# Slots on both sides of the dense blocks, earlier return of the output weights' buffers, earlier projections

## The chip, the cores and the metric

The kernel runs on one core of a Trainium2 chip. The metric is the device time of one launch in microseconds. Engines are named as the profile names them: PE (TensorE matmul) and PEld (its weight load), DVE (VectorE), ACT (ScalarE), POOL (GpSimd) and SP (SyncE, which here only issues transfers).

## The reference

All data is float32, 2048 tokens of width 512. The output is `x + A(xn) + B(xn)` with `xn = layernorm(x)`.

```python
# A: 32 heads of width 16, one shared key and value head
q = (xn @ wq).reshape(B, S, H, Dh).transpose(0, 2, 1, 3); k = xn @ wk; v = xn @ wv
p = softmax(einsum("bhqd,bkd->bhqk", q, k) * Dh ** -0.5)
A = einsum("bhqk,bkd->bhqd", p, v).transpose(0, 2, 1, 3).reshape(B, S, H * Dh) @ wo
# B: product-key experts, 64 x 64 of them, 32 heads
q1, q2 = split(einsum("nd,dhc->nhc", xn, w_q))            # 128 wide each
t1, i1 = top2(q1 @ k1.T); t2, i2 = top2(q2 @ k2.T)
top_s, top_e = top2(t1[:, None] + t2[None, :])            # of the 4 candidates
g = softmax(top_s)
act = gelu(einsum("nd,nhkd->nhk", xn, u[top_e]))          # tanh form
B = einsum("nhk,nhk,nhkd->nd", g, act, v[top_e])
```

So each token has 64 experts (32 heads, two each) out of 4096.

## The kernel before

**Attention sets the pace.** Tokens are 16 tiles of 128, in four groups. After a start stage (norms, transposes, projections) the main loop runs over `half` = 256 pairs `d` and a few more. A pair is two chunks of 128 keys for one unit; a unit is one block of 512 queries and four heads, so a unit is 8 pairs and a query block 64. Query blocks come in the order `QB = (0, 1, 3, 2)`. In a pair PE makes scores (`scores`, L325), ACT their exponentials (L328), and PE the products with the values (`pv`, L339). `i = 2 * d` counts chunks.

**The order is written out by hand.** Inside the loop every engine executes its instructions in the order in which the program emits them. `att_steps` emits, for each pair: stored-up transfers, half of the scores, the value products of the pair before, then `mid`, the other half of the scores, at most one output projection, and `fill`. `fill` advances the score thread, a generator whose yields carry costs, up to a budget that grows evenly over the loop.

**Experts are done in two ways.** Token groups 0 and 1 gather expert rows: this work is cut into 512 slots (`NSL`), each one expert of one token tile. A slot is a gather of 128 rows of 1024 floats by POOL (L957), a dot with the tokens on DVE (L969), and, four slots at a time, a short gate chain (L978 to L980 on DVE, tanh L985 on ACT, weight L992), then a weighted add into the token tile on DVE (L1004). Groups 2 and 3 are done densely, each in a dense block of the score thread: the last routing items (scores L527, top values L540 and L542, `batch` L567 to L639), transposes of the routing (L744), a one-hot stage that builds gate matrices (DVE L767 to L770, PE L801, ACT L806, then transfers to and from `d_g`), and 32 dense steps of activations (L719), GELU and gate on DVE and ACT (L886 to L907), and sums over experts (PE L843, DVE L846).

**Stages of a dense block.** `dense_on` is 0 outside; 3 from the third routing item of the block's last chunk; 2 from the end of the routing transposes, that is in the one-hot stage; 3 again from two steps before the one-hot stage's end; 1 from the end of dense step 4; and 0 when the block ends.

**Pace of the slots.** `pos` is the number of slots due. Each pair adds to it by the stage, `todo` is what of it is not yet dotted, and `mid` emits those dots, then a limited number of adds (`sums`), then up to four gathers.

```python
if d < half * 3 // 4:
    pos += 2.1 if len(IDX) < NC * TPH else (1.7, 2.5, 1.4, 0.0)[dense_on[0]]
else:
    pos += max(0.0, NSL - pos) / max(half - 4 - d, 1) if dense_on[0] < 3 else 0.0
```

**The gather ring.** Slots' rows lie in a ring of `NGB` = 12 buffers. `gathers` issues while `g_next < a_next + NGB - lent`, so a buffer comes free by a slot's add. The output weights `wo` of attention (two buffers' worth) borrow from the same ring: `lent` becomes 2 at `i % 128 == 124` (pairs 62, 126, 190), and `load_wo` loads them a few pairs into the next query block.

**Output projections.** `block_out` (PE L432, DVE add L436) projects one token tile of a finished query block; there are four to a block. For blocks 0 and 2 of the order two are emitted in the dense block (steps 2 and 3), the others from `i % 128 >= HOLD` on; for block 1 they come at every other pair as soon as the tiles are in place. Each charges 3.6 to the score thread's budget. `lent` returns to 0 at `HOLD + 8` (for block 1 at 30), and the last 30 chunks have the limit reduced once more.

Of the kernel before, what the change touches and what calls it, by code (L numbers as in the profile page):

```python
# [33 lines left out]
NC = 8  # L34
TPH = GT
# [11 lines left out]
LIMIT2 = 25000.0  # L47
C_IN = 0.7978845608028654
C_CUB = 0.044715 * C_IN
HOLD = 56  # L50
MOST = 4.0
UNIT = 0.235

# [2 lines left out]
def tile_kernel(ctx, tc, x, wq, wkv, wo, wqT, kT, uv, ub, vb, out):  # L56
# [246 lines left out]
    def load_q(u, rows=True, maxima=True):  # L303
        qb, hg = units[u]
        qa = qa_bufs[u % 2]
        QA[u] = qa
        c = slice(qb * 512, (qb + 1) * 512)
        for b in range(2):
            h0 = 4 * hg + 2 * b
            o = 64 * b  # L310
            if maxima:
                nc.sync.dma_start(raw(qa[o + 48:o + 50]), d_m[:, h0:h0 + 2, c])
            if rows:
                src = [d[h0 * DH:(h0 + 2) * DH, c].rearrange("(h r) n -> r h n", r=DH) for d in (d_qh, d_ql)]
                nc.sync.dma_start(raw(qa[o:o + 16]), src[0])
                nc.sync.dma_start(raw(qa[o + 16:o + 32]), src[0])
                nc.sync.dma_start(raw(qa[o + 32:o + 48]), src[1])
# [3 lines left out]
    def scores(u, kc, i):  # L321
        p = stile("sc")
        for b in range(2):
            o = 64 * b
            nc.tensor.matmul(p[:, b, :], kaug[o:o + 64, kc * P:(kc + 1) * P], QA[u][o:o + 64, i, :],  # L325
                             start=True, stop=True)
        pt = late[0].tile([P, 2, 512], F32, name="pt", tag="pt", bufs=6)
        nc.scalar.activation(pt, p, AF.Exp, scale=SCALE)  # L328
        PT[u, kc, i] = pt

    def pv(u, kc):
        if kc == 0:
            pv_t = ps.tile([P, 512], F32, name="pv", tag="pv", bufs=1)
            PV[u] = pv_t
        for i in range(2):
            pt = PT.pop((u, kc, i))
            for b in range(2):
                j = 2 * b + i
                nc.tensor.matmul(PV[u][32 * j:32 * j + 32, :], vaug[:, kc, :], pt[:, b, :],  # L339
                                 start=kc == 0, stop=kc == 15)  # L340
# [51 lines left out]
    WO, lent = [], [0]  # L392
# [33 lines left out]
    def block_out():  # L426

        m, j = PWO.pop(0)
        t = GT * QB[m] + j
        p = xtile("pwo")  # L430
        for k in range(KC):
            nc.tensor.matmul(p, ON[4 * m + k][:, j * P:(j + 1) * P], WO[k // 2][:, k % 2, :],  # L432
                             start=k == 0, stop=k == KC - 1)
        assert t in LIVE
        acc = ACC[t]
        behind(lambda: nc.vector.tensor_add(acc, acc, p))  # L436
        DONE_A[t] = True

    def out_ready():
        return PWO and GT * QB[PWO[0][0]] + PWO[0][1] in LIVE  # L440
# [106 lines left out]
    IDX, G = {}, {}  # L547
# [398 lines left out]
    NSL = len(slots)  # L946
# [93 lines left out]
    def run(fns):  # L1040
        todo = fns[:]
        fns.clear()
        for fn in todo:
            fn()
# [55 lines left out]
    dense_on = [0]  # L1100
# [3 lines left out]
    def run_scores(until=None, key=None):  # L1104
        while (until is not None and spent[0] < until) or (key is not None and key not in IDX):
            posts()
            try:
                cost = next(sgen)
            except StopIteration:
                spent[0] = 1e9  # L1110
                posts()
                return
            if cost is None:

                if key is None:
                    return
                continue
            spent[0] += cost

    STEPS = 512  # L1120


    def att_steps(d, mid, fill):
        i = 2 * d
        run(STORES)
        if 144 <= i < STEPS and i % 128 == 16:
            PWO.extend((i // 128 - 1, j) for j in range(4))
        if i < STEPS:
            u, kc = divmod(i, 16)
            if i == 0:  # L1130
                load_q(0, rows=False)
                run_scores(until=spent[0] + 6.0)
            if kc == 4 and u + 1 < 32:
                load_q(u + 1)
            scores(u, kc, 0)
            scores(u, kc, 1)
        if 0 < i <= STEPS:
            pu, pk = divmod(i - 2, 16)
            pv(pu, pk)
            pv(pu, pk + 1)  # L1140
            if pk == 14:
                unit_tail(pu)
        mid()
        if i < STEPS:
            scores(u, kc + 1, 0)
            scores(u, kc + 1, 1)
        if out_ready() and (i % 128 >= HOLD and PWO[0][0] != 1 or i % 4 == 0 and PWO[0][0] == 1):
            block_out()
            spent[0] += 3.6
        fill()  # L1150

        pp, r = divmod(i, 32)
        if pp and pp < 16:
            if r == 4:
                pair_load(pp - 1)
            if r == 6:
                pair_invert(pp - 1)
            if r == 10:
                pair_spread(pp - 1)
            if r == 12:  # L1160
                pair_tail(pp - 1)
        if i == STEPS - 4:
            for j in range(3):
                last_out_a(j)
        if i == STEPS + 2:
            last_out_a(3)
            last_out_b()
        if i >= 124 and i % 128 == 124 or i == STEPS - 30:
            lent[0] = 2
        if i >= 128 and i % 128 == 10 or i == STEPS - 10:  # L1170
            load_wo()
        if i == STEPS - 6:
            load_last()
        if i >= 128 and i % 128 == (30 if 256 < i < 384 else HOLD + 8):
            lent[0] = 0


    xs = [[load_x(j, True) for j in range(GT)]]
# [51 lines left out]
    with tc.manual_schedule(engines={E_.PE, E_.Activation, E_.DVE, E_.Pool, E_.SP}):  # L1230
        done0 = spent[0]
        half = STEPS // 2
        pos = 0.0
        for d in range(half + 24):


            if d < half * 3 // 4:
                pos += 2.1 if len(IDX) < NC * TPH else (1.7, 2.5, 1.4, 0.0)[dense_on[0]]
            else:
                pos += max(0.0, NSL - pos) / max(half - 4 - d, 1) if dense_on[0] < 3 else 0.0  # L1240

            todo = max(min(int(pos + 0.001), g_next[0]) - d_next[0], 0)

            def mid():
                post = POST[:]
                POST.clear()
                for act, _ in post:
                    act()
                tanhs(d_next[0])
                run(ON_ACT)  # L1250
                ON_ACT.extend(LATER_ACT)
                LATER_ACT.clear()
                run(LAST)
                LAST.extend(LATER)
                LATER.clear()
                rest = BEHIND[:]
                BEHIND.clear()

                dots(d_next[0] + todo - 1)
                if a_ready[0] > a_next[0]:  # L1260
                    weigh(a_next[0] // SB)
                dots(d_next[0] + 1 if todo > 0 else 0)
                for _, fn in post:
                    fn()
                sums = min(a_ready[0] - a_next[0], max(todo, 3) if d < half else 4)
                if dense_on[0] == 3:
                    sums = min(sums, 1)
                if dense_on[0] == 2:
                    run(CHAIN)

                def go():
                    n = sums
                    while rest or CHAIN or n > 0:
                        if n > 0:
                            adds(1)
                            n -= 1
                        elif not rest:
                            run(CHAIN)
                        if CHAIN:
                            CHAIN.pop(0)()  # L1280
                        if rest:
                            rest.pop(0)()
                    gathers(4)
                    if OUTS:
                        experts_out(OUTS.pop(0))

                if dense_on[0] == 2:
                    POST_FILL.append(go)
                else:
                    go()  # L1290

            aim = done0 + (FILL - done0) * (d + 1) / half if d < half else 1e6

            def fill():
                run_scores(until=min(aim, spent[0] + MOST))
                run(POST_FILL)

            att_steps(d, mid, fill)
        flush()
        run(STORES)  # L1300
        while a_next[0] < NSL:
            dots(NSL)
            run(CHAIN)
            tanhs(d_next[0])
            adds(SB)
            run(STORES)
            gathers(NGB)
        assert not OUTS
        run(STORES)
# [37 lines left out]
```

## Time and profile before

| | us |
|---|---|
| median of three runs | 2026.66 (2023.86 to 2029.93) |
| the profiled execution's time | 2021.49 |
| its span, first to last instruction | 2019.8 |
| PE busy | 1888.2 (93%) |
| DVE busy | 1679.9 (83%) |
| ACT busy | 1293.9 (64%) |
| POOL busy | 571.2 (28%) |
| mean granted PE clock | 0.968 |

The shares are means over stages with different limits. A stretch of the loop is read in a window: each engine's busy time in it, the granted clock, and the share in which the 16 DMA engines moved data. An engine that is busy nearly all of a stretch bounds it; where none is, the table of waits says who waited for whom.

### The profile page before, as it was taken

How to read it: one execution, taken by the hardware profiler on the slowest of the kernel's cores; microseconds unless marked ns; L12 is line 12 of the kernel's file. 1: busy time of each engine (PE TensorE's matmuls, PEld its weight loads, DVE VectorE, ACT ScalarE, POOL GpSimd, SP SyncE). 2: the span in 40 equal slices, each digit the busy share in tenths (PEclk: the TensorE clock that was granted, in tenths of full speed). 3: DMA queues.
4: the chain of work that ended last, by engine and by line, in shares of the span. 5: the costliest groups of instructions: out<-in, count | busy, mean ns of one | idle time of the engine just before them, and what ended most of it. 6: DMA issues, size and time to landing. Idle time of an engine off the chain costs nothing.

```text
span 2019.8 us, 34706 instructions
## 1 busy us (share of the span) xinstructions
PE 1888.2 (93%) x10990; PEld 1001.1 (50%) x10990; DVE 1679.9 (83%) x6713; ACT 1293.9 (64%) x1801; POOL 571.2 (28%) x540
## 2 busy tenths in 40 slices
PE   6869999999999999999999999999998987899987
PEld 3634444555555544555554454555454544455542
DVE  6536888999998957899997799999888577899992
ACT  3336666555558877888785555555776765577763
POOL 2202322222221312334433222122123133445430
PEclk9989999999999899999999999999987998999998
DMA  7757787986654875888879777676378666889972
GB/s 275 290 211 250 250 295 266 321 297 224 235 189 112 231 219 179 274 269 269 283 244 368 237 265 270 224 254 201 102 206 269 194 215 226 273 295 320 305 261 78
DMA packets 238041, 492.16 MB, mean 244 GB/s; under 512 B 93204, under 2 KB 93204, under 8 KB 237852
## 3 DMA queue, kind: packets, MB, share of 16 engines
q0 software_dynamic: 73728, 268.47, 39.9%
q1 hardware_dynamic: 162120, 219.82, 33.1%
q10 hardware_dynamic: 2004, 1.61, 0.3%
q8 instruction: 88, 1.44, 0.3%
q14 instruction: 101, 0.83, 0.1%
HBM read 428.46 MB, written 56.07 MB: 240 GB/s over the span
## 4 chain that ended last, share of the span: by engine, by line
PE 48%; DVE 30%; DMA 8%; issue 4%; ACT 2%; POOL 1%; SPq 0%; ACTq 0%; DVEq 0%; POOLq 0%
PE pv L339 14%; PE sc L325 9%; PE psc L527 9%; DVE xa L1004 6%; DVE g L969 5%; PE pout L843 5%; PE pact L719 5%; DVE i L542 5%; DMA g<-in_uv_dram,idx 4%; DVE m L540 3%; PE pg L801 2%; PE pw L482 2%; PE pwo L432 1%; ACT pt L328 1%; DVE oh L767 1%
## 5 line engine op out<-in xcount | busy, mean ns | idle before, releaser
L328 ACT ACTIVATE pt<-sc 128x1024 f32<-128x1024 f32 x1024 | 992.5, 1025 | 476.6 <-PE sc L325 440.4
L957 POOL DMA_INDIRECT g<-in_uv_dram,idx x512 | 558.2, 1090 | 1382.9 <-DVE xa L1004 694.3
L339 PE MATMUL pv<-pt,vaug 128*32 128x512 f32 x4096 | 518.2, 624 | 0.0
L325 PE MATMUL sc<-qa,kaug 64*128 64x512 f32 x2048 | 388.5, 454 | 15.3 <-ACT pt L328 14.4
L527 PE MATMUL psc<-wk,xt 128*128 128x512 f32 x1536 | 389.2, 401 | 6.9 <-DMA xt<-dxt 2.3
L1004 DVE SCALAR_TENSOR_TENSOR xa<-g,w,xa 128x512 f32<-128x512 f32 x512 | 372.2, 747 | 0.1
L969 DVE CUSTOM_DVE_ANT_0 g<-g,xa 128x512 f32<-128x512 f32 x512 | 336.1, 685 | 35.3 <-DMA g<-in_uv_dram,idx 35.3
L527 PEld LDWEIGHTS psc<-wk,xt 128*128 128x128 f32 x1536 | 277.4, 188 | 111.5 <-issue 44.4
L325 PEld LDWEIGHTS sc<-qa,kaug 64*128 64x128 f32 x2048 | 157.8, 187 | 338.5 <-ACT pt L328 213.1
L843 PE MATMUL pout<-wk,wd 128*128 128x512 f32 x768 | 205.5, 416 | 36.0 <-DVE gy L886 18.8
L339 PEld LDWEIGHTS pv<-pt,vaug 128*32 128x32 f32 x4096 | 109.9, 112 | 259.5 <-issue 257.9
L542 DVE FIND_INDEX8 i<-m,psc 128x8 uint32<-128x64 f32 x1024 | 207.0, 225 | 0.0
L719 PE MATMUL pact<-xt,wk 128*128 128x512 f32 x768 | 196.6, 400 | 4.5 <-DVE da L846 1.4
L843 PEld LDWEIGHTS pout<-wk,wd 128*128 128x128 f32 x768 | 146.1, 196 | 88.3 <-DVE gy L886 22.1
L540 DVE MAX8 m<-psc 128x8 f32<-128x64 f32 x1024 | 146.5, 217 | 29.7 <-PE psc L527 27.0
L719 PEld LDWEIGHTS pact<-xt,wk 128*128 128x128 f32 x768 | 139.2, 188 | 54.5 <-issue 19.4
L684 DVE TENSOR_TENSOR wk<-rw,wk 128x512 fp32r<-128x512 f32 x128 | 85.1, 686 | 21.1 <-ACT wk L683 21.1
L846 DVE TENSOR_TENSOR da<-da,pout 128x512 f32<-128x512 f32 x128 | 82.9, 682 | 11.5 <-PE pout L843 11.4
L801 PE MATMUL pg<-oh 128*128 128x32 f16 x1024 | 74.2, 246 | 7.4 <-DVE oh L770 6.6
L801 PEld LDWEIGHTS <-oh 128*128 128x128 f16 x1024 | 69.3, 164 | 20.1 <-issue 11.0
L767 DVE TENSOR_TENSOR oh<-oh 128x2048 f16<-128x2048 f16 x64 | 78.0, 1219 | 0.0
L683 ACT CAST wk<-rw 128x512 fp32r<-128x512 f32 x128 | 73.8, 627 | 4.8 <-DMA rw<-in_ub_dram 3.7
(155 smaller groups left out, 1297.5 us busy)
## 6 DMA issues: line engine op xcount, KB each, us to landing
wk<-dw SPq DMA_DIRECT2D x96, 512.0 KB
wqt<-in_wqT_dram SPq DMA_DIRECT2D x32, 512.0 KB
dw<-wk SPq DMA_DIRECT2D x32, 512.0 KB
rw<-in_ub_dram SPq DMA_DIRECT2D x64, 256.0 KB
rw<-in_vb_dram SPq DMA_DIRECT2D x64, 256.0 KB
gy<-dg SPq DMA_DIRECT2D x64, 256.0 KB
dg<-gst SPq DMA_DIRECT2D x30, 512.0 KB
qa<-dqh SPq DMA_DIRECT2D x128, 64.0 KB
```

The source lines that it names most:

```text
L325: nc.tensor.matmul(p[:, b, :], kaug[o:o + 64, kc * P:(kc + 1) * P], QA[u][o:o + 64, i, :], start=True, stop=True)
L328: nc.scalar.activation(pt, p, AF.Exp, scale=SCALE)
L339: nc.tensor.matmul(PV[u][32 * j:32 * j + 32, :], vaug[:, kc, :], pt[:, b, :], start=kc == 0, stop=kc == 15)
L527: nc.tensor.matmul(p, XT[g][k][:, a, j * P:(j + 1) * P], WC[n_][k][:, bb, :], start=n == 0, stop=n == 11)
L540: nc.vector.max(m8[:, jb, s, :], p[:, s * E:(s + 1) * E])
L542: nc.vector.max_index(i8[:, jb, s, :], m8[:, jb, s, :], p[:, s * E:(s + 1) * E])
L719: nc.tensor.matmul(p, us[:, a, k * P:(k + 1) * P], XT[DG][k][:, c, :], start=n == 0, stop=n == 11)
L801: nc.tensor.matmul(p[:, i * NB:(i + 1) * NB], oa[:, :, i], ob[:, :, i], start=True, stop=True)
L843: nc.tensor.matmul(p, wd[0][:, a, j * P:(j + 1) * P], vs[:, c, :], start=n == 0, stop=n == 5)
L957: nc.gpsimd.indirect_dma_start(out=gt, out_offset=None, in_=uv, in_offset=bass.IndirectOffsetOnAxis(ap=IDX[ph, c, ti][:, s:s + 1], axis=0))
L969: nc.vector.tensor_tensor_reduce(u, u, XN[TPH * ph + ti], scale=1.0, scalar=0.0, op0=OP.mult, op1=OP.add, accum_out=a[:, i:i + 1])
L1004: nc.vector.scalar_tensor_tensor(acc, v, w[:, i:i + 1], acc, op0=OP.mult, op1=OP.add)
```

## The change

Four things. The rates of slots change: pairs in `dense_on` 3 get 1.5 slots instead of none; scoring pairs get 1.75 instead of 1.7, and 2.3 in the twelve pairs behind a dense block; the first block's dense stage gets 2.6 instead of 2.5. From pair 192 on, only the dense stage spreads what is left (to one pair later than before), and the one-hot stage keeps 1.4. At most two adds instead of one are emitted in a pair of `dense_on` 3. `HOLD` falls from 56 to 44, so the third and fourth projections of blocks 0 and 2 move from pairs 92, 93 and 220, 221 to 86, 87 and 214, 215. And `lent` returns to 0 when the fourth projection of a block is emitted, no longer at a fixed chunk.

```diff
-HOLD = 56
+HOLD = 44
...
         behind(lambda: nc.vector.tensor_add(acc, acc, p))
         DONE_A[t] = True
+        if j == 3:
+
+            lent[0] = 0
...
-        if i >= 128 and i % 128 == (30 if 256 < i < 384 else HOLD + 8):
-            lent[0] = 0
...
-        pos = 0.0
+        pos, since = 0.0, half
         for d in range(half + 24):
 
 
-            if d < half * 3 // 4:
-                pos += 2.1 if len(IDX) < NC * TPH else (1.7, 2.5, 1.4, 0.0)[dense_on[0]]
+            if dense_on[0] != 0:
+                since = d
+            if dense_on[0] == 1:
+                pos += 2.6 if d < half * 3 // 4 else max(0.0, NSL - pos) / max(half - 3 - d, 1)
             else:
-                pos += max(0.0, NSL - pos) / max(half - 4 - d, 1) if dense_on[0] < 3 else 0.0
+                pos += (2.1 if len(IDX) < NC * TPH else 2.3 if 0 <= d - since < 12 else 1.75, 0, 1.4, 1.5)[dense_on[0]]
...
                 if dense_on[0] == 3:
-                    sums = min(sums, 1)
+                    sums = min(sums, 2)
```

## The prediction

> **What bounds the kernel now.** I read the page first (engine shares, slices, costliest groups), then cut the main loop into stretches and read each engine's busy time in them, then the waits inside the worst stretch.
>
> ```profile
> span 2019.8 us, 34706 instructions
> PE 1888.2 (93%) x10990; PEld 1001.1 (50%) x10990; DVE 1679.9 (83%) x6713; ACT 1293.9 (64%) x1801; POOL 571.2 (28%) x540
> ...
> PE   6869999999999999999999999999998987899987
> ...
> DVE  6536888999998957899997799999888577899992
> ...
> PEclk9989999999999899999999999999987998999998
> ...
> L957 POOL DMA_INDIRECT g<-in_uv_dram,idx x512 | 558.2, 1090 | 1382.9 <-DVE xa L1004 694.3
> ...
> L1004 DVE SCALAR_TENSOR_TENSOR xa<-g,w,xa 128x512 f32<-128x512 f32 x512 | 372.2, 747 | 0.1
> L969 DVE CUSTOM_DVE_ANT_0 g<-g,xa 128x512 f32<-128x512 f32 x512 | 336.1, 685 | 35.3 <-DMA g<-in_uv_dram,idx 35.3
> ...
> L801 PE MATMUL pg<-oh 128*128 128x32 f16 x1024 | 74.2, 246 | 7.4 <-DVE oh L770 6.6
> ```
>
> TensorE is the bound: it is busy 93%, and the holes lie in slices 30 to 36, about 1480 to 1820 us. A slot (one gathered expert row per token) costs one gather on POOL (L957) and, on DVE, a dot (L969) and a weighted add (L1004): 0.685 + 0.747 = 1.43 us.
>
> The loop has 256 pairs of key chunks. A pair begins with every eighth of the 2048 score matmuls, and that is how I placed the stretches. The program has two dense blocks of like content, 119 pairs apart: pairs 62 to 133 and 181 to 252. The next rows are windows over the first block: before its one-hot stage (two rows), one-hot with pairs 65 to 72 and 73 to 81, its far side (82 to 88), then the dense stage (89 to 103, 104 to 130, 131 to 133). Columns: stretch, length, busy us of PE, PEld, DVE, ACT, POOL, granted clock, DMA share, GB/s.
>
> ```profile
> 587.70:606.30 18.60, 14.31 (x79) 7.72 (x79) 17.76 (x113) 9.57 (x11) 3.96 (x4) 0.93 0.40 135
> 606.30:616.20 9.90, 9.09 (x45) 4.37 (x44) 3.02 (x9) 6.02 (x9) 0.00 (x0) 0.79 0.08 17
> 616.20:660.70 44.50, 44.14 (x433) 24.49 (x432) 42.65 (x90) 40.29 (x66) 7.10 (x6) 0.96 0.58 150
> 660.70:715.60 54.90, 53.95 (x476) 27.33 (x474) 51.09 (x104) 45.49 (x78) 15.81 (x13) 0.88 0.81 228
> 715.60:768.60 53.00, 49.63 (x269) 24.05 (x269) 21.46 (x35) 38.16 (x52) 4.03 (x4) 0.97 0.65 187
> 768.60:872.90 104.30, 104.30 (x580) 54.89 (x579) 91.46 (x216) 80.23 (x112) 40.02 (x36) 1.00 0.76 247
> 872.90:1062.10 189.20, 188.71 (x1069) 104.29 (x1068) 177.05 (x412) 150.98 (x215) 73.92 (x67) 1.00 0.82 267
> 1062.10:1085.60 23.50, 21.67 (x123) 11.80 (x122) 19.88 (x47) 14.25 (x19) 9.42 (x9) 1.00 1.04 387
> ```
>
> The second block: one-hot with pairs 184 to 191 and 192 to 200, far side (201 to 208), dense stage (209 to 223, 224 to 250, 251 and 252).
>
> ```profile
> 1433.60:1442.50 8.90, 8.90 (x59) 4.99 (x58) 2.96 (x9) 6.02 (x10) 0.00 (x0) 0.84 0.00 0
> 1442.50:1492.20 49.70, 48.12 (x417) 24.15 (x416) 43.85 (x91) 40.07 (x67) 9.56 (x8) 0.86 0.60 160
> 1492.20:1557.50 65.30, 55.59 (x490) 29.94 (x488) 62.13 (x141) 47.66 (x82) 21.20 (x19) 0.86 0.84 246
> 1557.50:1616.50 59.00, 57.66 (x302) 27.97 (x300) 31.50 (x60) 42.43 (x56) 9.70 (x8) 0.96 0.65 206
> 1616.50:1755.80 139.30, 114.90 (x575) 60.44 (x574) 108.11 (x261) 81.62 (x116) 54.49 (x49) 0.91 0.71 233
> 1755.80:1954.40 198.60, 190.03 (x1069) 104.04 (x1068) 198.04 (x484) 151.27 (x218) 97.62 (x85) 1.00 0.91 303
> 1954.40:1976.00 21.60, 16.75 (x79) 7.91 (x78) 15.81 (x35) 9.50 (x13) 1.43 (x1) 0.84 0.40 135
> ```
>
> See three things. (1) 209 to 223 take 139.3 us where the same fifteen pairs of the first block (the same number of score, dense and projection pairs) take 104.3, with no engine full: DVE is busy 108 of 139. (2) 192 to 200 take 65.3 against 54.9. (3) In 224 to 250 DVE is busy 198.04 of 198.60: there it is the bound. The waits of 1616 to 1756 name the cause of (1):
>
> ```profile
> DVE g L969 <- DMA g<-in_uv_dram,idx: 29.8, 20, 2.8
> ...
> PE pout L843 <- DVE gy L886: 16.8, 5, 5.2
> ```
>
> DVE stands in its dots until gathers land, 29.8 of the 35.3 us that the whole run has of this wait; behind the dot in DVE's queue stands the dense block's GELU (L886), and TensorE's output sums (L843) wait for that. The gather ring is 12 buffers; from pair 190 the limit is 10, and it stays so until pair 224, where the stall ends. The other half of the cause is pace. Before, slots have no due rate on the sides of a block, and from pair 192 what is left is spread evenly over the pairs that may hold slots. By the formula 370.6 slots are due by pair 207, so 141.4 are left for 44 pairs: 3.21 a pair. The dots' own count agrees:
>
> ```profile
> L969 DVE CUSTOM_DVE_ANT_0 g<-g,xa x48: 622/692/695, 1617.2 to 1751.4; 128x512 f32<-128x512 f32 x48
> ```
>
> 48 dots in 15 pairs are 3.2. The first block runs at 2.5, with its limit also at 10 in pairs 89 to 95 and 126 to 133, and none of the 35.3 us falls there.
>
> **The change part by part.** No instruction is added or removed; slots, projections and buffer returns move. I ran the new rates by hand over the stages found above. Due slots by the end of pair 81: 148.0 (142.0 before); 88: 158.5 (142.0); 133: 275.5 (254.5); 180: 363.8 (334.4); 200: 392.1 (370.6); 207: 402.6 (370.6). Left for pair 208 on: 109.4 over 45 pairs, 2.43 a pair against 3.21, a little less than the first block's 2.5.
>
> *Gains, by the first block's same pairs.*
> Pairs 209 to 223: 139.3 - 104.3 = 35.0.
> Pairs 192 to 200: one-hot pace falls from 2.77 to 1.4, the first block's. 65.3 - 54.9 = 10.4, less sixteen one-hot matmuls that the second stretch has more (16 x 74.2 / 1024 = 1.2): 9.2.
> Pairs 224 to 250: 198.6 - 189.2 = 9.4.
> Block end: pairs 251 and 252 take 21.6, at the first block's 23.5 / 3 = 7.8 a pair 15.7. Bounds 0 and 5.9; the work differs and the tail follows, so I take the middle, 3.
> Pairs 184 to 191 (49.7 against 44.5) have the same pace in both blocks already: nothing.
> Sum of gains 56.6.
>
> *Costs.* Slots before the one-hot stage (pairs 62 to 64, 181 to 183):
>
> ```profile
> 596.28 0.74 DVE L1004 SCALAR_TENSOR_TENSOR xa<-g,w,xa 128x512 f32<-128x512 f32 x1
> ...
> 605.27 1.11 PE L744 MATMUL ptd<-ident,da 128*128 128x128 f32 x4 [3.88 <-DVE da L627]
> ...
> 1432.33 1.39 PE L744 MATMUL ptd<-ident,da 128*128 128x128 f32 x8 [2.44 <-DVE da L627]
> ```
>
> TensorE waits there for the routing chain on DVE, which is busy 17.76 of 18.60. The first pair's slots stand ahead of the chain: 1.5 dots and one add more are 1.5 x 0.685 + 0.747 = 1.8 us a block. The second and third pair's slots are issued behind the chain's last step, in a DVE busy 3.02 of 9.90: nothing. Bounds per block 0 and 4.5 x 1.43 = 6.4; I take 1.8, as the row's one add in front of the chain shows where they land: 3.6 in all.
>
> [...]
>
> Far sides (pairs 82 to 88, 201 to 207): 10.5 slots a block, 15.0 us of DVE, into 53.0 - 21.46 = 31.5 and 59.0 - 31.50 = 27.5 us of idle DVE. Bounds 0 and 15.0 each. The dots wait for nothing, since the ring is full there, but their adds release gathers beside the gate rows that the block is fetching: 1.5 each, 3 in all, near the hidden end because of the idle time.
>
> The wider stretches:
>
> ```profile
> 376.90:587.70 210.80, 208.32 (x1188) 115.48 (x1187) 202.64 (x1351) 120.79 (x149) 50.57 (x51) 1.00 0.76 258
> 768.60:817.20 48.60, 48.60 (x263) 24.21 (x262) 39.29 (x94) 35.35 (x48) 17.10 (x16) 1.00 0.65 211
> 1085.60:1169.80 84.20, 82.59 (x445) 40.25 (x444) 61.47 (x329) 48.10 (x56) 24.62 (x24) 1.00 0.82 285
> 1169.80:1415.70 245.90, 242.87 (x1383) 133.88 (x1382) 233.24 (x1548) 141.49 (x173) 56.19 (x56) 1.00 0.70 237
> 1616.50:1679.70 63.20, 52.57 (x276) 29.06 (x275) 49.21 (x120) 39.30 (x57) 21.64 (x20) 0.92 0.67 219
> ```
>
> Scoring at 1.75 instead of 1.7: 1.5 slots in pairs 32 to 61 (2.1 us, DVE idle 8.2) and 1.8 in 146 to 180 (2.5 us, idle 12.7). Bounds 0 and 4.6; I take 0.5. The twelve pairs behind the first block at 2.3: 7.2 slots, 10.3 us in an idle DVE of 22.7: nothing, 10.3 at most. Dense stage at 2.6: 4.5 slots, 6.4 us, idle DVE 12.8 + 12.2: bounds 0 and 6.4, I take 1. Slot 256 is reached some eight pairs sooner, so the two loads each of four token tiles move from the block's end, where DMA is at 1.04, into its dense stage. They pass the weight and gate fetches on SP, where they wait for an output store:
>
> ```profile
> SPq L1064 <- DMA out_dram<-xa: 11.8, 3, 5.8
> ```
>
> At worst 11.8 us of waiting for fetches that run two blocks ahead, at best some 2.5 saved in the crowded end (23.5 against 3 x 189.2 / 27 = 21.0): 0.
>
> *Projections and buffers.* Two projections of block 0 move from pairs 92 and 93 to 86 and 87, two of block 2 from 220 and 221 to 214 and 215. Each is eight matmul records and one DVE add (block 2's four, in the row below, are 32 records), and charges the score thread the same 3.6 as before, so that TensorE's other work slides two pairs later and is even again by 94 and 222: nothing. No DMA is issued by them.
>
> ```profile
> L432 PE MATMUL pwo<-wo,on x32: 592/592/697, 1570.7 to 1732.2; 128*128 128x512 f32 x32
> ```
>
> The limit returns to 12 in pair 87 and 215 instead of 96 and 224; for block 1 in 142 instead of 143. The next gathers into those two buffers wait on POOL for the projection's matmuls and then run. With the limit at 10 and 2.5 a pair showing no wait in the first block, the return alone is worth little at 2.43; it insures pairs 216 to 223, and I count it inside the 35.0.
>
> Costs: 3.6 + 3 + 0.5 + 1 = 8.1. Net 56.6 - 8.1 = 48.5. The profiled execution took 2021.49, so 1973; it lies 5.2 under the median of the three runs, 2026.66, against which I predict: 1978.
>
> **The rivals.**
> A: the starvation stays in part. For it: the gathers could be late by DMA latency and the adds' groups of four rather than by the ring and the pace, and pairs 209 to 215 still have a limit of 10. Against it: the first block's 89 to 95, no gather wait. Price: those seven pairs keep 63.2 - 48.6 = 14.6, giving 1993; if all 35.0 stays, 2014. All of it is still faster.
> B: DVE's work is the same and only changes place; if all 30 slots put on the sides were bare, 30 x 1.43 = 42.9 us would eat the gain: 2022, no change. It needs the two idle DVE stretches (31.5 and 27.5) to be useless.
> C, slower: the same slots are bare and stand in DVE's queue ahead of work that TensorE waits for, so that each of the 20 side pairs also costs clock. It decides from 48.5 / 20 = 2.4 us a side pair on, which is 1.6 slots bare and nothing hidden. At 4 us a pair it gives 2026.66 - 56.6 + 80 = 2050. For it: TensorE does wait for DVE in pairs 62 and 181, and fetches are late in 82 to 84. Against it: in the side rows DVE has 60 us idle and POOL is almost still.
>
> **How the numbers follow.** Forecast 0.70, own range 1963 to 1991 (low: nothing exposed, the block end at its 5.9 and pairs 184 to 191 at the first block's 44.5, 56.6 + 2.9 + 5.2 = 64.7 of gain, 1962; high: half the far sides' 30 us shows, 12 more than taken); A 0.18; B 0.06; C 0.06. The measurement tells about 0.3%, 6 us, from no change. Faster: forecast and A and a part of B, 0.90; same 0.05; slower 0.05. The range leaves out the far half of A, B and C: 1963 to 2004.
>
> **What would show it.** Right: pairs 209 to 223 in about 105 us with almost no dot waiting for a gather; DVE under 95% in the last 27 dense pairs; one-hot pairs 192 to 200 near 56; far sides as long as before with DVE about 15 us busier. Wrong: the 29.8 us wait still there (A), the far sides or pairs 62 and 181 longer by several us with TensorE waiting on DVE (B, C), or scoring pairs lengthened beyond the mean of 210.8 / 30 = 7.03 us of pairs 32 to 61 because DVE overflows.

## The result and the profile after

The changed kernel takes 1971.55 us (median of four runs, 1964.6 to 1981.35), the kernel before beside it 2027.24: a ratio of 0.973, 95% interval 0.9685 to 0.9775. Timed again later, on the chip of some of the experiments, it took 1974.05 (ratio 0.9745, 0.9708 to 0.9781). Comparisons of stretches below are between profiled executions: 2021.49 before, 1969.9 after.

The page of the changed kernel: the span, the engines, TensorE's, VectorE's and the clock's slices, and the gather and the dot (lines stand three further on than before).

```profile
span 1968.2 us, 34715 instructions
PE 1871.4 (95%) x10990; PEld 993.5 (50%) x10990; DVE 1678.5 (85%) x6713; ACT 1291.5 (66%) x1801; POOL 563.0 (29%) x540
...
PE   6879999999998998999999999999989899999997
...
DVE  6527888999998975899999789999989878899993
...
PEclk9989999999998899999999999999988899999998
...
L960 POOL DMA_INDIRECT g<-in_uv_dram,idx x512 | 550.1, 1074 | 1342.9 <-DVE xa L1007 703.0
...
L972 DVE CUSTOM_DVE_ANT_0 g<-g,xa 128x512 f32<-128x512 f32 x512 | 335.5, 680 | 1.0 <-DMA g<-in_uv_dram,idx 0.9
```

VectorE does the same work (1678.5 us against 1679.9), but its 35.3 us of waiting for gathers are 0.9, and the holes of TensorE in slices 33 to 35 are gone. What holes remain lie at the two blocks' sides. Windows over the same pairs as before: the near side (62 to 64), the far side (82 to 88), then of the second block the near side (181 to 183), one-hot (192 to 200), far side (201 to 208) and the dense stage (209 to 223, 224 to 250, 251 and 252). Columns as before: stretch, length, busy us of PE, PEld, DVE, ACT, POOL, granted clock, DMA share, GB/s.

```profile
589.70:619.30 29.60, 22.54 (x124) 11.99 (x123) 27.15 (x159) 14.94 (x20) 8.27 (x7) 0.88 0.41 130
721.20:781.30 60.10, 53.37 (x258) 22.48 (x258) 32.30 (x74) 36.28 (x50) 15.76 (x15) 0.91 0.78 239
...
1425.10:1455.50 30.40, 24.94 (x141) 13.54 (x141) 25.68 (x138) 16.27 (x22) 6.60 (x6) 0.89 0.44 135
1505.10:1560.50 55.40, 50.22 (x490) 27.87 (x488) 50.32 (x103) 45.70 (x77) 11.66 (x11) 0.92 0.78 217
1560.50:1617.80 57.30, 57.24 (x300) 27.79 (x299) 39.39 (x87) 43.73 (x62) 14.48 (x14) 0.96 0.77 245
1617.80:1721.50 103.70, 103.70 (x577) 54.28 (x576) 91.19 (x218) 80.18 (x113) 41.31 (x38) 1.00 0.81 266
1721.50:1910.30 188.80, 188.80 (x1069) 104.39 (x1068) 178.50 (x412) 150.44 (x214) 76.11 (x67) 1.00 0.82 270
1910.30:1924.60 14.30, 14.09 (x81) 7.54 (x80) 12.06 (x30) 9.29 (x12) 0.00 (x0) 1.00 0.52 181
```

From pair 209 to 252 TensorE is now busy all the time; VectorE's share in 224 to 250 is 94.5% (178.50 of 188.80) where it was 99.7% and the bound. The stretch that lost most is the first block's far side: 60.1 us against 53.0.

### The profile page after: what moved, and what is told of

It reads as the page before. It is cut to its first block, busy times and chain, and to the rows that moved or that the text cites. A ratio compares the mean times of both kernels' runs of the same rounds, so it can differ in the third digit from the quotient of the medians.

```text
span 1968.2 us, 34715 instructions
## 1 busy us (share of the span) xinstructions
PE 1871.4 (95%) x10990; PEld 993.5 (50%) x10990; DVE 1678.5 (85%) x6713; ACT 1291.5 (66%) x1801; POOL 563.0 (29%) x540
## 4 chain that ended last, share of the span: by engine, by line
PE 65%; DVE 19%; DMA 5%; ACT 2%; issue 2%; SPq 0%; ACTq 0%; DVEq 0%
PE pv L339 19%; PE sc L325 13%; PE psc L530 9%; PE pout L846 9%; PE pact L722 9%; DVE i L545 5%; DVE m L543 3%; DVE xa L1007 3%; PE pg L804 3%; DVE g L972 3%; ACT pt L328 2%; PE pwo L432 2%; PE pw L485 1%; DMA dg<-gst 1%; DMA wqt<-in_wqT_dram 1%
## 5 line engine op out<-in xcount | busy, mean ns | idle before, releaser
L960 POOL DMA_INDIRECT g<-in_uv_dram,idx x512 | 550.1, 1074 | 1342.9 <-DVE xa L1007 703.0
L1007 DVE SCALAR_TENSOR_TENSOR xa<-g,w,xa 128x512 f32<-128x512 f32 x512 | 371.2, 744 | 0.0
L846 PE MATMUL pout<-wk,wd 128*128 128x512 f32 x768 | 195.4, 402 | 2.8 <-DVE wd L904 2.7
L846 PEld LDWEIGHTS pout<-wk,wd 128*128 128x128 f32 x768 | 140.6, 188 | 50.8 <-DVE act L972 5.1
L995 DVE SCALAR_TENSOR_TENSOR w<-gth,ga 128x4 f32<-128x4 f32 x128 | 20.2, 158 | 84.9 <-ACT gth L988 84.6
```

What stands on the lines that cost most here:

```text
L846: nc.tensor.matmul(p, wd[0][:, a, j * P:(j + 1) * P], vs[:, c, :], start=n == 0, stop=n == 5)
L960: nc.gpsimd.indirect_dma_start(out=gt, out_offset=None, in_=uv, in_offset=bass.IndirectOffsetOnAxis(ap=IDX[ph, c, ti][:, s:s + 1], axis=0))
L1007: nc.vector.scalar_tensor_tensor(acc, v, w[:, i:i + 1], acc, op0=OP.mult, op1=OP.add)
```

## The experiments

Three questions: what cured the starvation of pairs 209 to 223 (the buffers' return, the pace, or something that both act on), why the first far side lost, and whether more is to be had. Each starts from the kernel before (here called B) or the changed one (A); where one of the prediction's rivals is meant, the word rival stands with its letter.

**1. Buffers and projections alone.** B, with the change's `HOLD` and return, and the written rates as before.

```diff
-HOLD = 56
+HOLD = 44
...
+        if j == 3:
+            lent[0] = 0
```

> The kernel before with only the projections' move (HOLD 44) and the buffers' return behind the fourth projection; the pace of slots is the old one. Theory (pace first, ring second): pairs 209 to 215 starve as before (63 us), since the limit is still 10 and the pace still 3.2; from pair 216 on the limit is 12, where pairs 224 to 250 of the kernel before ran 7.4 us a pair without gather waits, so 216 to 223 fall from 76 to about 60 us: 2010. Rival (the ring alone is the cause): nearly the whole 35 us comes back, 1992. Rival (gathers are late by the DMA engines, the ring is beside the point): 2027, no change.

Measured 2054.26, ratio 1.0103 (1.0062 to 1.0144): slower than before, which none of the theories had. Rows of the windows 209 to 223 and 224 to 250, and of its waits:

```profile
1626.60:1757.00 130.40, 113.46 (x577) 59.97 (x576) 107.31 (x263) 81.31 (x117) 54.97 (x49) 0.91 0.75 248
1757.00:1985.10 228.10, 202.15 (x1069) 112.08 (x1068) 201.11 (x485) 151.46 (x217) 96.53 (x86) 0.93 0.80 265
...
DVE g L972 <- DMA g<-in_uv_dram,idx: 56.8, 39, 3.9
```

The first fifteen pairs gain 8.9 us, the 27 that follow lose 29.5, though up to pair 240 all 12 buffers are back, as they are there in B too. So a ring of 10 was not the cause by itself. The pace did not stay quite the same: by the program's order the earlier projections move the start of the first block's dense stage from pair 89 to 91, two pairs lose their slots, and 3.30 slots a pair are left for the end instead of 3.20.

**2. Pace alone.** A, with `HOLD = 56` and the return at the fixed chunk.

```diff
-HOLD = 44
+HOLD = 56
...
-        if j == 3:
-            lent[0] = 0
...
+        if i >= 128 and i % 128 == (30 if 256 < i < 384 else HOLD + 8):
+            lent[0] = 0
```

> The changed kernel with the old projections (HOLD 56) and the old return of the buffers; the new pace is kept. Theory (pace): at 2.43 slots a pair a limit of 10 does not starve, so pairs 209 to 223 stay near 104 us and the time is that of the changed kernel, 1968 to 1976. Rival (the earlier return is needed): pairs 216 to 223 stall again by up to 20 us, 1990.

Measured 1981.86, ratio 0.9751 (0.9721 to 0.9782). The time lies above the 1968 to 1976 expected, but so did the kernel before beside it (2030.44); the ratio is that of A's repeat, 0.9745.

```profile
1636.20:1739.70 103.50, 103.50 (x575) 54.26 (x574) 92.46 (x218) 80.55 (x113) 42.14 (x38) 1.00 0.82 263
1739.70:1928.50 188.80, 188.80 (x1069) 104.37 (x1068) 174.45 (x403) 150.02 (x213) 72.14 (x64) 1.00 0.80 262
...
DVE g L969 <- DMA g<-in_uv_dram,idx: 2.6, 3, 1.5
```

The second dense stage is as in A. Pace carries the gain; the buffers' return and the earlier projections add nothing there.

**The quantity behind both: the lead.** A gather needs the buffer that an add frees: of POOL's 1342.9 us of idle time before gathers in A, 703.0 end with an add (L1007), more than with anything else. How far the gather then stands ahead of its dot is the ring less the slots by which the dots lead the adds. From the records of POOL's gathers and DVE's dots (k-th gather with k-th dot) I worked out the lead when the gather starts, in slots, and the median time from a gather's start to its dot:

| kernel | pairs 209–215 | 216–223 | 224–247 |
|---|---|---|---|
| before | 2.3 slots, 6.1 us | 2.1, 6.4 | 3.8, 10.3 |
| after | 3.6, 10.2 | 5.1, 17.3 | 5.5, 17.1 |
| 1 buffers alone | 2.5, 6.3 | 3.0, 8.5 | 2.8, 9.1 |
| 2 pace alone | 4.2, 13.2 | 3.5, 11.4 | 5.5, 17.0 |
| 3 buffers, more adds | 2.5, 6.7 | 3.9, 10.3 | 4.9, 12.1 |
| 5 ten buffers, new pace | 1.4, 6.2 | 3.2, 10.7 | 3.5, 11.2 |

In the kernels of the table whose dots wait, the shortest time from a gather's start to its dot is 4.4 to 4.8 us. Wherever the median is 9.1 us or less, dots wait; at 12 and more there are next to no waits; between them both occur. A dot that waits starts when its gather has landed, so a short median is in part the waiting itself; what the experiments set from outside is the pace, the adds and the buffers. The adds' records give the other term: in 224 to 247 the dots run 8.1 slots ahead of the adds before, 6.4 after, 9.1 in (1) and 6.9 in (3), the slot whose add has just freed the buffer counted in; with the lead that makes the 12 buffers each time (8.1 + 3.8, 6.4 + 5.5, 9.1 + 2.8, 6.9 + 4.9). At 3.3 slots a pair the written limit, three adds or as many as dots, does not let the adds of (1) catch up: of the two buffers that pairs 216 to 223 got back, 0.9 became lead, and in 224 to 247 the lead is 1.0 shorter than before with the same buffers. Experiments 3 to 5 test this.

**3. (1) with more adds.** From pair 216 up to 4 adds a pair.

```diff
-  sums = min(a_ready[0] - a_next[0], max(todo, 3) if d < half else 4)
+  sums = min(a_ready[0] - a_next[0], max(todo, 3 if d < 216 else 4) if d < half else 4)
```

> The kernel before with the change's buffers and earlier projections alone (as in the run with those alone, 2054), and besides up to 4 adds a pair from pair 216 on where there were 3. In the order written, the adds then no longer stay 7 slots behind the dots, and the gathers stand 4 to 9 slots ahead of the dots where they stood 5 (3 from pair 241). Theory (what starves is a lead of the gathers under about two pairs of dots): pairs 224 to 250 fall from 228 to 190 to 200 us, the waits of dots on gathers from 57 us to under 30, the time to 2010 to 2025. Rival (at 3.3 slots a pair the gathers themselves cannot keep up, whatever the lead): 224 to 250 stay at 215 to 230 and the time at 2045 to 2055.

Measured 2023.36, ratio 0.9993 (0.996 to 1.0026).

```profile
1743.90:1948.20 204.30, 193.90 (x1069) 106.12 (x1068) 203.60 (x498) 151.59 (x218) 96.39 (x88) 0.98 0.88 300
...
DVE g L972 <- DMA g<-in_uv_dram,idx: 30.2, 15, 4.4
```

31 us faster than (1) with the same pace and buffers, and none of the 30.2 us of waits falls behind 1744: what cost (1) its 27 pairs was the lead. The stretch does not come down to 190 to 200, because without waits VectorE is full, 203.60 of 204.30. So the old pace has a second price that no buffer removes.

**4. A tighter limit in the order.** A, with `lent` at 4 in pairs 209 to 223.

```diff
+        if 418 <= i < 448:
+            lent[0] = 4
+        if i == 448:
+            lent[0] = 0
```

> The changed kernel with 8 instead of 10 to 12 buffers allowed to the gathers in pairs 209 to 223, all else as it is: the gathers stand 3 to 4 slots ahead of the dots (1.2 to 1.6 pairs at 2.46 slots a pair) where they stood 5 to 8. Theory (the lead in pairs decides): the dots wait on gathers again, 10 to 30 us more in these 15 pairs, 104 us becomes 114 to 134, the time 1982 to 2000. Rival (the slower pace alone cured it): under 5 us more, 1970 to 1980.

Measured 1975.22 (0.9712 to 0.9804), beside 1974.05 of A on the same chip: no effect, but no verdict for the rival either. The leads are A's to the tenth (3.6 slots, 10.4 us; 5.1, 17.3). POOL does hardly anything but gathers (550.1 of its 563.0 us in A), and its longest waits are here, too, the gathers' for the adds (697.3 us, `POOL g L960 <- DVE xa L1007`); gathers that are emitted later in the program started as early as in A. `lent` orders; it did not throttle.

**5. Ten real buffers.** A, with `NGB = 10`.

> The changed kernel with 10 gather buffers instead of 12 in all (8 while the output weights hold two), nothing else changed. In the run with a tighter limit in the order alone, GpSimd issued its gathers as early as before, so that only buffers that are really there can tighten the ring. By the order written the gathers of pairs 209 to 215 then stand 3 to 4 slots ahead of the dots (1.2 to 1.6 pairs at 2.46 slots a pair), from 216 on 5 (2.0 pairs). Theory (the lead in pairs decides): dots wait on gathers 8 to 30 us in all, above all in pairs 207 to 215, which take 54 to 62 us where they took 48; the time is 1980 to 2000. Rival (the slower pace alone cured it): waits under 4 us, the time 1969 to 1980.

Measured 2002.3, ratio 0.9886 (0.9855 to 0.9918), 28 us over A. Waits of dots in the whole run, in 1085 to 1190 us (pairs 132 to 144) and in 1640 to 1752 (209 to 223):

```profile
DVE g L972 <- DMA g<-in_uv_dram,idx: 61.7, 33, 5.8
...
DVE g L972 <- DMA g<-in_uv_dram,idx: 27.3, 10, 5.8
...
DVE g L972 <- DMA g<-in_uv_dram,idx: 18.3, 11, 2.9
```

At the new pace the starvation is back: 209 to 215 take 56.3 us for 47.9, 216 to 223 62.1 for 55.8. The waits are twice the most that I expected and the time lies just above its range, since I had not seen that 134 to 145, where the lead falls to 1.7 slots, would starve too. Pace alone is no cure; the lead is what decides, and pace, adds and buffers all act on it.

**6. The first block at its old rates.** A, but with the old rates and one add until pair 133.

```diff
-            if dense_on[0] == 1:
+            if d < half // 2 + 6 and dense_on[0] != 0:
+                pos += (0, 2.5, 1.4, 0.0)[dense_on[0]]
+            elif dense_on[0] == 1:
...
-                    sums = min(sums, 2)
+                    sums = min(sums, 2 if d > half // 2 else 1)
```

> The changed kernel, but up to the end of the first dense block the old rates (no slots on its sides, 2.5 in its dense stage, 1.7 in scoring, one add on its sides). About 21 slots move to later pairs: by the formula 2.88 a pair are left for the second dense stage. Theory: the first block gets back the 10 us that the changed kernel lost there (pairs 62 to 94), and the second dense stage, with DVE at about 7.1 us of work a pair against 6.9, loses some 11 us, with gather waits of 0 to 10 us in pairs 209 to 215: 1971 to 1982, and a dot-to-gather wait between those of 2.43 and 3.21. Rival (only side slots of the second block matter): 1961.

Measured 1990.09, ratio 0.9791 (0.9754 to 0.9827). Pairs 82 to 88 take 49.7 us, some 10 less than in A, and 216 to 223 take 65.9 with 13.3 us of waits for gathers in the run, since the slots left out come there: 2.99 a pair by the program's order, not the 2.88 that I had worked out, and the time misses the 1971 to 1982 expected. So slots on the first block's sides do relieve the end, and cost about 10 us where they stand.

**What the far side waits for.** SP's store of the first gates (L812) and their fetch behind it (L679) in A, what VectorE did then, and what it waited for in 721 to 790:

```profile
733.11 0.38 SPq L812 DMA_DIRECT2D dg<-gst  x1
742.25 2.19 SPq L679 DMA_DIRECT2D gy<-dg  x3
...
733.98 0.75 DVE L1007 SCALAR_TENSOR_TENSOR xa<-g,w,xa 128x512 f32<-128x512 f32 x1
745.15 0.69 DVE L896 SCALAR_TENSOR_TENSOR gy<-gy 128x512 f32<-128x512 f32 x1 [10.42 <-DMA gy<-dg]
...
DVE gy L896 <- DMA gy<-dg: 11.9, 2, 10.4
...
DVE w L995 <- ACT gth L988: 9.3, 1, 9.3
```

The fetch follows the store 9.1 us later (3.4 before), VectorE stands 10.4 us for it, and behind VectorE stand ScalarE's casts and then its exponentials, so that TensorE has no work: pair 84 lasts 11.8 us. Eight gathers of 0.5 MB each start between 720 and 735; before there are four, all by 721. In the repeat of A a second wait stood out, too: ScalarE's `wd <- dg<-gst`, 6.3 us, for buffers that the later stores of the gates had not yet given back, with VectorE's slot weights waiting 10.1 us behind ScalarE.

**7 and 8. Gathers left out of the order there.** A, with none emitted in pairs 81 to 84 and 200 to 203, then (8) in pairs 81 to 87 of the first block alone.

```diff
-                    gathers(4)
+                    gathers(0 if quiet[0] > 0 else 4)
```

> The changed kernel, but no gathers are issued in four pairs (81 to 84 and 200 to 203), while the gate matrices are stored to and fetched from memory; dots and adds go on. Theory (the far side's loss is the gathers' transfers in front of the gate store and fetch): the fetch of the gates in the first block starts some 3.5 us behind the store, as before, not 9.1; pairs 82 to 93 get back about 6 us: 1965. Rival (the loss is the dots and adds on VectorE, or the projections' move into this stretch): no change, 1971.

> The changed kernel with no gathers issued from pair 81 to 87 of the first dense block, so that none lie beside the store and the fetch of the gates there; the slots of pairs 81 to 84 are fed by those already landed, those of 85 to 88 come later, up to 4 a pair in 89 and 90. Theory (the gathers hold up the store of the gates and their fetch, for which VectorE waits 10.4 us in its order, with the softmax behind it): the fetch follows the store within 5 us, the wait falls under 5 us, pairs 82 to 88 take 50 to 54 us where they took 60, and the time falls by 4 to 8 us. Rival (the slots' own VectorE work does it): pairs 82 to 85 as long as before, and what 86 to 88 gain, 89 to 91 lose; the time within 2 us of the changed kernel.

Measured 1982.61 (ratio 0.976, 0.9717 to 0.9802) and 1969.94 (0.9741, 0.9698 to 0.9785); 82 to 88 take 60.4 and 63.2. Both fail as tests, for the reason seen in (4). In (8) the gathers from slot 153 on are emitted in pair 88, which begins at 775.9 us, and later; on the chip slot 153 starts at 723.12 all the same, and slots 158 and 159 start here, over twenty us ahead of that pair:

```profile
750.76 0.94 POOL L961 DMA_INDIRECT g<-in_uv_dram,idx  x1 [14.94 <-DVE xa L1008]
752.50 1.14 POOL L961 DMA_INDIRECT g<-in_uv_dram,idx  x1 [0.80 <-DVE xa L1008]
```

**9. Gathers really held.** As (8) but from pair 80 on, and a POOL copy of eight columns of the fourth block of gates stands ahead of the later gathers.

```diff
                 fetched.add(b)
+                if b == 3 and d_next[0] < NSL // 2:
+                    nc.gpsimd.tensor_copy(small.tile([P, 8], F16, name="after_g", bufs=1), gate_rows(3)[:, :8])
```

> The changed kernel, first dense block alone changed: gathers from slot 150 on stand behind a small GpSimd copy that reads the fourth block of gates, so that on the chip none can start between the last gathers of pairs 80 to 82 and the landing of that fetch; the slots of pairs 83 to 88 come later, 4 a pair from 89 on, and the dots may wait on gathers there (1 pair of lead). Theory (eight gathers of the slots, 4 MB, hold up the store of the gates, their fetch and the return of the store's buffers): the fetch follows the store within 5.5 us, the wait of VectorE for the gates falls from 7 to 12 us to 5 to 6, pairs 82 to 88 take 50 to 54 us where they took 60 to 64; 89 to 95 lose some 3 to 12 of it again. Rival (VectorE's own work for the slots): pairs 82 and 83 as long as in the changed kernel (18 to 23 us together), since their dots and adds are still there; only 84 to 88 gain.

Measured 1982.54, ratio 0.9768 (0.9739 to 0.9797); the profiled execution is the longest of the four, 1996.74.

```profile
740.76 0.38 SPq L814 DMA_DIRECT2D dg<-gst  x1
743.48 1.28 SPq L679 DMA_DIRECT2D gy<-dg  x3
...
754.11 0.19 POOL L682 CAST after_g<-gy 128x8 f16<-128x8 f32 x1 [38.03 <-DMA dinv<-rc]
754.85 1.39 POOL L963 DMA_INDIRECT g<-in_uv_dram,idx  x1 [0.55 <-DVE xa L436]
...
ACT wd L903 <- DMA dg<-gst: 8.4, 1, 8.4
DVE w L998 <- ACT gth L991: 5.0, 1, 5.0
DVE gy L899 <- DMA gy<-dg: 0.5, 1, 0.5
```

(The copy reads the fourth block of gates, whose fetch was issued at 749.87; the row names another transfer as what ended its wait.) With no gathers beside it the fetch follows the store in 2.7 us, VectorE's wait for the gates is 0.5 us, and pairs 82 to 85 take 29.2 us (39.0 in A, 35.9 in its repeat). But the gathers set free at 754 meet the last store of the gates (issued at 757.2), ScalarE waits 8.4 us for its buffers, and 86 and 87 take 23.6 us. The total of 82 to 88 stays at 60.4, and the bunched slots lose 7 us in 89 to 93. Its theory holds for the store and the fetch, and its sum for 82 to 88, 50 to 54, does not: the cost comes up again where the gathers and the last store meet.

**10. No slots on the first far side.** A with rate 0 in pairs 82 to 90, 2.6 instead of 2.3 in 134 to 145, the rest of the slots at the end.

> The changed kernel without slots behind the one-hot stage of the first dense block (pairs 82 to 90), which costs 13 slots there; 3.6 of them go into pairs 134 to 145 (2.6 a pair for 2.3), the others into the last stage (2.7 a pair for 2.46). If the slots there cost what the changed kernel shows (60 to 64 us for pairs 82 to 88, against 50 to 54 without): these pairs take 50 to 54, pairs 209 to 250 lose 0 to 4 us with the higher pace, and the time is 1962 to 1971, 4 to 10 us under the changed kernel. Rival (the 10 us only move: the slots cost the same later, as VectorE and the gathers are near their limit there): 209 to 250 grow by 6 us or more and the time is 1970 to 1980.

Measured 1968.2, ratio 0.971 (0.9687 to 0.9734). 82 to 88 take 59.1: the dots and adds are gone, but POOL still fills the buffers that are free: eight gathers start between 717.2 and 737.0 us, as eight do in A, and the fetch follows the store by 6.9 us. Pairs 209 to 250 cost no more at the higher pace (292.5 us, A 292.5). The slots' own VectorE work is not the cost. In 134 to 145, at 2.6 slots a pair, the median from a gather's start to its dot is 8.8 us and dots wait 8.5 us, but these pairs take 82.5 us as in A (82.4).

**11. No slots, and gathers held until the stores have landed.** As (10) with 2.7 in the first dense stage and 2.3 behind it, and as (9), with the copy reading the fourth weighted tile `wd`, which needs a buffer of the stored gates.

```diff
                 nc.scalar.copy(wd[0][:, 0, :], y)
+                if b == 3 and d_next[0] < NSL // 2:
+                    nc.gpsimd.tensor_copy(small.tile([P, 8], F16, name="after_g", bufs=1), raw(wd[0][:, 0, :8]))
```

> The kernel with the bare far side once more (no slots in pairs 82 to 90 of the first dense block), and with the gathers held there too: those from slot 150 on stand behind a small GpSimd copy of the weighted gates' fourth tile, which cannot be written before the store of the gates has given back its buffers, so that they start about pair 88, before the dots resume in pair 91. In place of the slots there, 2.7 a pair for 2.6 in pairs 91 to 133 and 2.66 for 2.46 from 207 on. Theory (gathers beside the store and the fetch of the gates are what the far side costs): the fetch follows the store within 5 us, VectorE waits under 5 us for the gates and ScalarE under 3 for the store's buffers, pairs 82 to 88 take 47 to 52 us (59 with bare slots alone, 60 to 64 in the changed kernel), the time is 1958 to 1968. Rival (the far side's length is set by the chain of dense work, not by the gathers): 82 to 88 stay at 56 to 60 and the time at 1968 to 1976. The higher pace may cost up to 6 us in pairs 91 to 133 (VectorE 96 per cent busy there at 2.6).

Measured 1963.24 (1960.18 to 1969.01), ratio 0.9688 (0.9658 to 0.9718): the lowest median here, against 0.9745 (0.9708 to 0.9781) of A's repeat; the intervals overlap by a thousandth, so a gain over A of the whole time is not quite shown, that of the stretch is. Window 82 to 88, SP, POOL, and what VectorE still waited for:

```profile
723.40:773.30 49.90, 48.68 (x259) 21.61 (x258) 21.86 (x40) 35.63 (x48) 10.37 (x11) 1.00 0.78 246
...
731.73 0.38 SPq L812 DMA_DIRECT2D dg<-gst  x1
734.68 1.27 SPq L679 DMA_DIRECT2D gy<-dg  x3
...
755.23 0.71 POOL L903 CAST after_g<-wd 128x8 f16<-128x8 f32 x1 [43.32 <-ACT wd L901]
756.10 1.23 POOL L963 DMA_INDIRECT g<-in_uv_dram,idx  x1 [0.15 <-DVE wd L907]
...
DVE gy L897 <- DMA gy<-dg: 2.2, 2, 2.0
```

The far side is 10 to 14 us shorter than in A, at full clock, and ScalarE has no wait for the stores' buffers left in it. Some of it is lost at the block's end (131 to 133: 27.2 for 21.5 to 24.1), where a reciprocal waits 3.3 us for its transfer (0.4 in A's repeat, 5.2 in (10)); what sets that was not tried.

Over all profiles here, 82 to 88 take 49.7 to 54.4 us in the five whose store meets at most four gathers and whose later stores meet none (before, 1, 3, 6, 11), and 59.1 to 64.2 in the nine in which eight gathers meet the stores (A, its repeat, 2, 4, 5, 7 to 10). What in the gathers does it, their bytes, their pieces or their queue, was not tried.

**12. A once more**, beside (3), (4) and (8).

> The changed kernel itself, beside the others of this call, as their base: about 1971 to 1980, ratio to the kernel before 0.97 to 0.978. Pairs 209 to 223 near 104 us, 82 to 88 near 60, 251 to 252 near 14.3.

Measured 1974.05, ratio 0.9745 (0.9708 to 0.9781). 82 to 88 take 64.2, 209 to 223 103.7, 251 and 252 14.2: the first is the one that scatters.

## Why the prediction was right, point by point

**Pairs 209 to 223**: 35.0 predicted, 35.6 measured (139.3 to 103.7). The step, that this stage would come to look like the first block's, held. The explanation in it was half right. That a limit of 10 and a pace of 3.21 starve the ring, and 2.43 does not, is what (2) shows (by the program's order the paces are 3.20 before, 2.41 in (2) and 2.46 in A, whose dense stage begins two pairs later than the prediction took it); behind it stands the lead, for which the dots' distance from the adds counts as much as the buffers (1, 3, 5). "The return alone is worth little" was too kind, since at the old rates the two moves together cost 1% (1), and that the return insures 216 to 223 is not borne out: without it they take 55.4 for 55.8 (2).

**Pairs 192 to 200**: 9.2 predicted, 9.9 measured. **224 to 250**: 9.4 predicted, 9.8 measured; VectorE full was read rightly, as (3) shows from the other side.

**Block end**: 3 predicted with an upper bound of 5.9, 7.3 measured (21.6 to 14.3). The bound came from the first block's end, 7.8 us a pair, which is no clean model: it measures 21.3 to 29.4 in the runs here. What the runs show in its place is the pace: the end takes 21.3 to 22.3 us in the three kernels at 3.2 to 3.3 slots a pair (before, 1 and 3) and 20.3 at 2.99 (6), but 14.2 to 15.3 at 2.69 and less (A, 2, 10, 11). It goes with the term before it: where VectorE is 99% busy in 224 to 250 (before, 3, 6), I take its work to be still behind when the block ends; TensorE waits there for the weights that VectorE makes, 4.8 us before and 0.2 in A:

```profile
PE pout L843 <- DVE wd L901: 4.8, 2, 2.6
...
PE pout L846 <- DVE wd L904: 0.2, 1, 0.2
```

**Near sides**: 1.8 each predicted, 1.1 and 3.6 measured, 4.7 for 3.6 in sum. The idle in front of the first block's routing transposes grew from 3.88 to 6.25 us, as the step had it; in the second it grew only from 2.44 to 3.05, and what set that block's 3.6 us stays open (the clock over pairs 181 to 183 fell from 0.94 to 0.89):

```profile
608.92 1.11 PE L747 MATMUL ptd<-ident,da 128*128 128x128 f32 x4 [6.25 <-DVE da L630]
...
619.30:666.80 47.50, 45.98 (x435) 24.92 (x434) 43.94 (x88) 40.42 (x66) 8.34 (x7) 0.93 0.67 176
```

The second row is pairs 65 to 72, 3.0 us longer than before at a clock of 0.93 (0.96 before). Over the runs that length does not go with the idle in front: the same pairs take 49.4 us at 0.86 in (6), whose near side has no slots, 46.2 at 0.93 in (1), whose idle is 3.92, and 46.0 at 0.96 in (7), whose idle is 6.26; in the kernel before, the second block's like pairs, 184 to 191, take 49.7 at 0.86 behind an idle of 2.44. So I cannot tell these 3.0 us from scatter.

**Far sides**: this is the term that was mis-sized: 1.5 each predicted within 0 to 15, measured 7.1 in the first block (11.2 in A's repeat), and a gain of 1.7 in the second. The sentence named the right neighbours, "their adds release gathers beside the gate rows that the block is fetching", and then went by VectorE's idle time for the price. That idle time was not free room. In the kernel before, VectorE's waits in 715.6 to 768.6 are headed by these:

```profile
DVE wk L684 <- ACT wk L683: 14.6, 4, 4.6
...
DVE gy L893 <- DMA gy<-dg: 5.4, 2, 5.1
```

Part of it, 5.4 us, is a wait for that very fetch, and it became 11.9 in A. The sign named for the far sides, as long as before with VectorE some 15 us busier, failed in the first block: 7.1 us longer, VectorE 10.8 us busier (32.30 for 21.46). (9), (10) and (11) show that the gathers are the price and the slots' arithmetic is not.

**Dense stage, scoring, phase-2 loads, twelve pairs behind the block**: 1.5 predicted together. Measured: 104 to 130 +0.1, 131 to 133 +0.6, 0 to 61 +1.0, 134 to 145 -1.8, 158 to 180 -1.9. Nothing here tells itself from scatter.

The sum: 51.6 us of span gained for 48.5 forecast, and 1971.55 for 1978. The gains were 62.6 for 56.6, the block end being most of the difference, and the far side's excess took most of that back; two errors offset each other, so that the time came so near is in part luck. The rivals fell: of rival A's 14.6 us nothing is left, and the side pairs cost 10 us in all (13 with pairs 65 to 72), not the 43 of rival B or the 80 of rival C. The clock, on which rival C counts, is as before in two of the four side stretches (0.88 in pairs 62 to 64, 0.96 in 201 to 208) and went from 0.97 to 0.91 in 82 to 88 and from 0.94 to 0.89 in 181 to 183; how much of those 10 us is the clock's, no run separates.

## What to carry to other kernels

Size a prefetch ring by its lead in time: buffers less what the consumer's last step lags behind its first, over the consumer's pace, and compare that with the transfer's own time under the load of that stage; here 9.1 us and less starved and 12 were enough. Before work is put into an engine's idle time, read what ends that idle time: if it is a transfer, new transfers beside it can make it longer, as here (5.4 us became 11.9). An engine that only issues gathers ran ahead of the written order here (4, 7, 8), so a limit in that order held nothing back; fewer real buffers (5) and a small operation that reads the awaited data (9, 11) did.

## What was not expected of the hardware

A store of 96 KB and the fetch behind it took 2.7 and 3.0 us from issue to issue with no gathers beside them (9, 11), 3.4 to 5.3 with four gathers around them (before, 1, 3, 6), and 5.1 to 10.3 with eight gathers started in the 15 to 20 us around (A, its repeat, 2, 4, 5, 7, 8, 10). This time alone does not give the far side: (4) and (5), at 5.2 and 5.1 us, have 61.3 and 63.0 us there, and in them ScalarE waits 4.9 and 6.4 us for the later stores' buffers, which is 1.6 at most in the kernels with four gathers.

Two buffers that came back nine pairs sooner in each dense block did not make a kernel faster by themselves (1): with the two moved projections and the slightly higher pace that followed from them the run lost 1%, and one more add a pair gave it back (3).
